# Heads regrouped into neighbouring sets, so that a chunk's projections and gathers split in two halves, in a two-part attention kernel bound by exponentials

## The chip, the cores and the metric

The kernel runs on one core of one Trainium2 chip. The metric is device time of one execution in microseconds (us), and less is better. Before the change it took 406.27 us, the median of 4 runs (405.89 to 406.65).

Five engines work at the same time, each through its own instructions in order: PE (matmul), DVE (VectorE), ACT (ScalarE, here nearly all exponentials), POOL (GpSimd) and SP, which in this kernel issues the DMA transfers. The rows `SPq` in the listings are the issuing of transfers by SP: they too go strictly one after another.

## The reference, cut to what matters

Two attention layers with 32 heads of 20 columns each read their own 2048 x 640 input. Their outputs are put side by side.

```python
# A: four segments of L = 512 rows, causal attention inside the segment plus a linear memory
for s in range(4):
    p = softmax(qs @ ks.T * scale + mask)          # 512 x 512 per head
    a_dot = p @ vs
    pq = phi(qs)                                   # phi(t) = t + 1 if t > 0 else exp(t)
    a_mem = (pq @ M) / (pq @ z + 1e-6)
    o = g * a_mem + (1 - g) * a_dot                # g = sigmoid(beta), one per head
    pk = phi(ks);  M += pk.T @ vs;  z += pk.sum()
A = o @ wo
# B: sliding window of 256 keys, causal
mask = (i - j >= 0) & (i - j < 256)
B = softmax(where(mask, q @ k.T * scale, -1e9)) @ v @ wo
out = concatenate([A, B], axis=-1)
```

## The kernel before

Work goes in eight chunks of 512 rows, in the order A0, B0, A1, B1, A2, B2, A3, B3; here they are called chunk 0 to chunk 7. In a chunk, eight groups of four heads are scored one after the other: PE writes scores `sc`, ACT turns them into exponentials `pt`, PE multiplies `pt` by v, and DVE transposes and normalises. While one chunk is scored, the projections of the next run in between.

A group's four heads lie in four bands of 32 partitions. Which heads make a group decides how much of q and k must exist before the group can be scored. Before, group g holds the heads g, 8+g, 16+g and 24+g:

```python
c0 = DH * (G * j + g)        # proj_direct (chunk 0): head 8j+g; DH = 20, G = 8
h = G * j + g                # the same in the products with v and in the memory
```

These four heads are spread over all 640 columns of q. For chunks 1 to 7 the projection is made in five column blocks of 128 (`m`). Each block is evicted by DVE to `st` and stored to DRAM by SP, then gathered back into the banded layout. The kernel can score no group before the last block has made this round trip:

```python
def bounce(self, m, st, scratch, dst, t, *key):
    def store():
        self.nc.sync.dma_start(out=scratch[m * P:(m + 1) * P, :], in_=st[:, m, :])
        ...                                        # tl: when the store should have landed
        if m > 0: f.at(tl - 150.0, spread)
    def spread():                                  # one gather per band j, four in all
        j = m - 1
        self.nc.sync.dma_start(out=dst[HD * j:HD * j + DH, :, :],
            in_=scratch[GW * j:GW * (j + 1), :].rearrange("(g d) s -> d g s", g=G))
        ...                                        # tl: when the gather should have landed
        if m == self.KT - 1: self.mark(tl, *key)   # only now q (or k) is "known"
...
key = (n, w, e[0]) if n == 0 else (n, w)           # what a score batch of chunk n waits for
need.append(self.done.get(key))
```

The order of the instructions is not written by hand. When the program is built, a small model of the engines' clocks (`Flow`) picks at each step the first thing in a list of jobs whose inputs should be there by then. The order on every engine, SP included, is fixed from then on.

Other parts that the change touches:

```python
# final_job: attention output -> DRAM, transposed back -> output projection -> ot -> DRAM
for tt in range(t0, t1):
    ot = self.wk.tile([P, 640], BF16, name="ot", bufs=2)        # two output buffers
    ...                                                         # 2 x (5 matmuls, eviction to ot)
    def store(ot=ot, r=r): nc.sync.dma_start(out=out2d[r:r + P, col:col + self.D], in_=ot[:])

# norm, chunks with memory: both halves in one multiply, then an add
u = self.wk.tile([P, 2, NB * DH], BF16, name="u", bufs=2)
nc.vector.tensor_tensor(out=self.u, in0=tv[...], in1=rr[...], op=ALU.mult)   # 128 x 640
nc.vector.tensor_tensor(out=dst, in0=self.u[:, 0], in1=self.u[:, 1], op=ALU.add)

# last chunk: every tile masked by a DVE multiply ("fd")
out.append([n, [(g, qt - 2, qt, 1, 0), (g, qt, qt, 1, 128), (g, qt - 1, qt, 1, 256)],
            [("fd", 0, 2)], []])

# start
get_x(0)                                        # transposing load of the first 512 rows
self.wk_A = self.load_w("wk_A", A_wk, pad=HD)
self.wq_A = self.load_w("wq_A", A_wq, pad=HD)
self.load_beta(A_beta)
```

The softmax here doesn't subtract the row's maximum and nothing guards it: scores larger than these inputs give would overflow.

## Time and profile before

| | before |
|---|---|
| time, median of 4 | 406.27 us |
| span of the profiled run | 404.9 us |
| granted PE clock, mean | 0.962 |
| busy: PE / DVE / ACT / POOL | 83 / 78 / 83 / 54 % |

The first lines of the page of before: busy time, share and instruction count of each engine. Below them are two rows that cut the span into 40 slices of 10.1 us, where a digit is the busy share in tenths.

```profile
PE 337.9 (83%) x4580; PEld 159.4 (39%) x4606; DVE 317.5 (78%) x643; ACT 335.4 (83%) x395; POOL 219.8 (54%) x448
...
ACT  1569990987899999998739999999899999999810
POOL 3245650896876677876517667878686664000000
```

PE and ACT have the same share, and the average does not say who bounds the kernel. The ACT row does: it reads 9 nearly everywhere, with dips in the first slices, at slice 6 (counting from 0), at 8 and 9, at 20 and at the end. ACT is saturated in between, so only the dips can be won. They add up to 404.9 - 335.4 = 69.5 us.

The ACT timeline of before names the dips. The columns are start, length, engine, line, operation, tiles and count. The bracket is the idle time before the row and what ended it.

```profile
15.36 9.27 ACT L439 ACTIVATE pt<-sc 128x1024 bf16<-128x1024 f32 x10 [2.67 <-PE sc L427]
27.77 3.77 ACT L439 ACTIVATE pt<-sc 128x1024 bf16<-128x1024 f32 x4 [3.14 <-PE sc L427]
...
70.50 1.51 ACT L439 ACTIVATE pt<-sc 128x768 bf16<-128x768 f32 x2 [9.54 <-PE sc L427]
...
93.90 5.36 ACT L439 ACTIVATE pt<-sc 128x768 bf16<-128x768 f32 x6 [4.43 <-PE sc L427]
```

```profile
207.48 1.94 ACT L439 ACTIVATE pt<-sc 128x1024 bf16<-128x1024 f32 x2 [7.85 <-PE sc L427]
```

```profile
380.75 5.73 ACT L439 ACTIVATE pt<-sc 128x768 bf16<-128x768 f32 x8 [0.83 <-PE sc L427]
```

The reader sees the first score exponential at 15.36 and 3.14 us lost at 24.6, where all of v was projected between two groups. Then 9.54 us are lost from 61 to 70.5 (chunk 1 waits for q), 4.43 us before 93.9, 7.85 us before 207.48, and small holes of 0.83 us in the last chunk. After the last row, 18.46 us pass without exponentials.

The waits of before. The columns are the waiting engine with its tile, what it waited for, the total, how many times and the longest.

```profile
PE m L588 <- DVE ot L594: 9.3, 7, 6.9
PE m L221 <- DMA wk_A<-in_A_wk_dram: 9.0, 1, 9.0
...
DVE ot L594 <- DMA out_dram<-ot: 8.1, 2, 6.5
...
PE m L352 <- DMA pkT<-scr_pk: 5.0, 1, 5.0
```

PE stood 9.0 us for the first weights and 5.0 us for the transposed `pkT`. It stood 6.9 us for DVE's evictions into `ot`, and DVE stood 6.5 us for an output buffer.

The issuing of transfers by SP in before, around the boundary of chunks 0 and 1 and around the hole at 199.6:

```profile
67.68 0.27 SPq L252 DMA_DIRECT2D qB<-scr_qB  x1
```

### The profile page before, as it was taken

Reading aid. Unit: us, or ns where it says so; the run is one execution under the profiler, and the core shown is the slowest. Engines: PE = TensorE matmul, PEld = TensorE weight load, DVE = VectorE, ACT = ScalarE, POOL = GpSimd, SP = SyncE. Lnnn points to the kernel's source line nnn. Section 1 sums busy time; section 2 is a strip of 40 time slices with the busy share of each in tenths; the row PEclk is TensorE's granted clock in tenths of the full one; section 3 lists DMA queues with packets and bytes.
Section 4 is the critical chain, followed back from the end, with each engine's and each line's share of the span. In section 5 each row is a group of like instructions: output and inputs, shape, how many; then the busy total and the mean of one; then the engine's idle time right before and its main releaser. Section 6 shows DMA issues by size and latency. Waiting matters only on the chain.

```text
span 404.9 us, 11529 instructions
## 1 busy us (share of the span) xinstructions
PE 337.9 (83%) x4580; PEld 159.4 (39%) x4606; DVE 317.5 (78%) x643; ACT 335.4 (83%) x395; POOL 219.8 (54%) x448
## 2 busy tenths in 40 slices
PE   1999988967889998887579989798899999998725
PEld 0444334323433443344334344343453344654412
DVE  5666798484897989799556898979867999999851
ACT  1569990987899999998739999999899999999810
POOL 3245650896876677876517667878686664000000
PEclk9999999995999999999869999999999999999986
DMA  7980344898646747155922765427545503173422
GB/s 224 257 300 2 93 127 108 181 190 204 142 126 167 169 111 177 57 169 141 165 82 75 192 161 141 114 87 187 157 115 150 156 24 90 64 177 83 83 70 63
DMA packets 102278, 54.50 MB, mean 135 GB/s; under 512 B 69328, under 2 KB 102224, under 8 KB 102224
## 3 DMA queue, kind: packets, MB, share of 16 engines
q1 hardware_dynamic: 102224, 53.76, 52.5%
q8 instruction: 36, 0.59, 0.6%
q14 instruction: 18, 0.15, 0.1%
HBM read 17.70 MB, written 23.59 MB: 102 GB/s over the span
## 4 chain that ended last, share of the span: by engine, by line
PE 39%; DVE 35%; DMA 10%; ACT 7%; issue 5%; SPq 3%; POOL 1%; DVEq 0%; ACTq 0%
PE m L269 10%; DVE tt L524 8%; PE sc L427 8%; ACT pt L439 7%; PE m L588 6%; PE m L486 5%; PE m L221 5%; PE m L391 5%; DVE st L275 4%; DVE pc L292 4%; DVE pt L455 3%; DVE ot L594 3%; DMA out_dram<-ot 3%; DVE o L544 2%; DVE e L291 2%
## 5 line engine op out<-in xcount | busy, mean ns | idle before, releaser
L439 ACT ACTIVATE pt<-sc 128x1024 bf16<-128x1024 f32 (+1 forms) x360 | 322.2, 1027 | 39.1 <-PE sc L427 38.5
L473 POOL TENSOR_SCALAR_AFFINE_SELECT pt<-pt 128x256 bf16<-128x256 bf16 (+1 forms) x304 | 160.9, 538 | 105.9 <-ACT pt L439 102.2
L524 DVE STREAM_TRANSPOSE tt<-m 128x512 f32<-128x512 f32 x88 | 60.8, 705 | 25.4 <-PE m L486 23.7
L470 POOL TENSOR_SCALAR_AFFINE_SELECT pt<-pt 128x256 bf16<-128x256 bf16 x128 | 62.1, 490 | 12.8 <-ACT pt L439 12.6
L275 DVE CAST st<-m 128x512 bf16<-128x512 f32 x70 | 47.5, 680 | 15.2 <-PE m L269 14.5
L427 PE MATMUL sc<-qB,kB 32*128 32x128 bf16 (+2 forms) x896 | 46.9, 256 | 7.4 <-ACT pt L439 6.2
L594 DVE CAST ot<-m 128x320 bf16<-128x320 f32 x64 | 30.7, 485 | 21.9 <-PE m L588 13.0
L588 PE MATMUL m<-wo_B,oT 128*128 128x320 bf16 x160 | 32.3, 340 | 16.3 <-DMA oT<-scr_o 7.9
L588 PEld LDWEIGHTS <-oT 128*128 128x128 bf16 x320 | 30.3, 103 | 39.6 <-issue 16.1
L391 PEld LDWEIGHTS <-xT 128*128 128x128 bf16 x320 | 29.3, 98 | 27.9 <-issue 17.0
L455 DVE TENSOR_TENSOR pt<-pt,fdmask 128x512 bf16<-128x512 bf16 x96 | 39.1, 433 | 0.0
L427 PE MATMUL sc<-qA,kA 32*128 32x128 bf16 (+3 forms) x512 | 33.5, 300 | 0.6 <-ACT pt L439 0.6
L391 PE MATMUL m<-wv_A,xT 128*128 128x320 bf16 x160 | 28.3, 305 | 6.2 <-DVE tt L524 3.1
L427 PEld LDWEIGHTS <-kB 32*128 32x128 bf16 x896 | 17.4, 92 | 39.8 <-issue 37.4
L588 PE MATMUL m<-wo_A,oT 128*128 128x320 bf16 x160 | 28.8, 305 | 4.6 <-DVE tt L524 2.0
L391 PE MATMUL m<-wBv,xT 128*128 128x320 bf16 x160 | 25.3, 299 | 3.4 <-DVE tt L524 1.5
L269 PE MATMUL m<-xT,wBq 128*128 128x512 bf16 x93 | 23.9, 379 | 2.6 <-DVE tt L524 0.8
L269 PE MATMUL m<-xT,wBk 128*128 128x512 bf16 x92 | 24.7, 381 | 1.2 <-DVE ot L594 0.3
L486 PE MATMUL m<-pt,vA 128*32 128x256 bf16 (+3 forms) x512 | 23.3, 302 | 1.3 <-DVE vB L406 0.8
L551 DVE TENSOR_TENSOR u<-tt,rr 128x640 bf16<-128x640 f32 x24 | 23.2, 965 | 0.5
L544 DVE TENSOR_TENSOR o<-tt,rr 128x320 bf16<-128x320 f32 x40 | 22.1, 553 | 1.1
L427 PEld LDWEIGHTS <-kA 32*128 32x128 bf16 x512 | 9.9, 92 | 31.9 <-issue 31.7
(62 smaller groups left out, 324.0 us busy)
## 6 DMA issues: line engine op xcount, KB each, us to landing
out_dram<-ot SPq DMA_DIRECT2D x32, 160.0 KB
scr_o<-o SPq DMA_DIRECT2D x28, 160.0 KB
scr_kB<-st SPq DMA_DIRECT2D x20, 128.0 KB
kB<-scr_kB SPq DMA_DIRECT2D x16, 160.0 KB
scr_qB<-st SPq DMA_DIRECT2D x20, 128.0 KB
qB<-scr_qB SPq DMA_DIRECT2D x16, 160.0 KB
scr_qA<-st SPq DMA_DIRECT2D x15, 128.0 KB
qA<-scr_qA SPq DMA_DIRECT2D x12, 160.0 KB
```

Source lines behind the costliest of these rows:

```text
L269: nc.tensor.matmul(ps[:, :], lhsT=w_ap[:, kt, m * P:(m + 1) * P], rhs=xT[:, kt, :], start=(kt == 0), stop=(kt == self.KT - 1))
L275: nc.vector.tensor_copy(out=st[:, m, :], in_=ps[:, :])
L391: nc.tensor.matmul(ps[:, 0:320], lhsT=xT[:, kt, tt * P:(tt + 1) * P], rhs=w_ap[:, kt, 320 * hf:320 * hf + 320], start=(kt == 0), stop=(kt ...
L427: nc.tensor.matmul(ps[j // 2][:, j % 2, c0:c0 + nq * P], lhsT=k[rows, g, P * kc:P * kc + P], rhs=q[rows, g, q0 * P:(q0 + nq) * P], start=T ...
L439: nc.scalar.activation(out=pt[:, :, lo:hi], in_=ps[i][:, :, lo:hi], func=ACT.Exp, scale=self.scale)
L455: nc.vector.tensor_tensor(out=pt[:, :, 0:256], in0=pt[:, :, 0:256], in1=self.fd[:].unsqueeze(1).to_broadcast([P, 2, 256]), op=ALU.mult)
L470: nc.gpsimd.affine_select(out=blk, in_=blk, pattern=pat, compare_op=ALU.is_ge, fill=self.zero, base=-1, channel_multiplier=1)
L473: nc.gpsimd.affine_select(out=blk, in_=blk, pattern=pat, compare_op=ALU.is_ge, fill=self.zero, base=0, channel_multiplier=-1)
L486: nc.tensor.matmul(O[HD * j:HD * j + HD, q0 * P:(q0 + nq) * P], lhsT=v[:, vt, VS * h:VS * h + HD], rhs=pts[j // 2][:, j % 2, c0:c0 + nq * ...
L524: self.nc.vector.transpose(out=tt[:, i, :], in_=O[:, :])
L588: nc.tensor.matmul(ps[:, 0:320], lhsT=oT[:, m, tt * P:(tt + 1) * P], rhs=wo[:, m, 320 * hf:320 * hf + 320], start=(m == 0), stop=(m == sel ...
L594: nc.vector.tensor_copy(out=ot[:, 320 * hf:320 * hf + 320], in_=ps[:, 0:320])
```

## The change

The intent is to let every chunk after the first begin when half of its heads are there. Head 4g+j takes the place of head 8j+g. Groups 0 to 3 are then the columns 0 to 319, so they need only the blocks m = 0, 1, 2, and groups 4 to 7 need the rest. Projections of q, k and v become half jobs, gathers come as four per half, and each group has its own mark. Around this core the change also:

- loads the first weights in two parts (352 of 640 columns first),
- carries the output weights through DRAM once to permute their rows,
- splits the normalisation of two-part groups into two multiplies and an add,
- gives the output three buffers,
- hands half of the last chunk's masks to POOL, as two selects each,
- changes some gates: phi of k no longer holds its store back until q of the next chunk is known, and k and q of the later B chunks now wait for phi of the chunk before,
- issues the small load of beta ahead of the weights, not behind them, and puts phi's two DVE operations into stretches where the clock model has DVE idle.

The diff, cut to this core:

```diff
-                c0 = DH * (G * j + g)
+                c0 = DH * (4 * g + j)
...
-            if m > 0:
+            if m in (2, 4):
                 f.at(tl - 150.0, spread)
         def spread():
-            j = m - 1
-            self.nc.sync.dma_start(
-                out=dst[HD * j:HD * j + DH, :, :],
-                in_=scratch[GW * j:GW * (j + 1), :].rearrange("(g d) s -> d g s", g=G))
+            g0 = 0 if m == 2 else 4
+            rows = scratch[4 * DH * g0:4 * DH * (g0 + 4), :]
+            for j in range(4):
+                self.nc.sync.dma_start(
+                    out=dst[HD * j:HD * j + DH, g0:g0 + 4, :],
+                    in_=rows.rearrange("(g j d) s -> j d g s", g=4, j=4)[j])
+            for g in range(g0, g0 + 4):
+                self.mark(tl, n, what, g)
...
+        for half in range(2):
+            for what, w, scr, dst in qk:
+                add(self.qk_job(n, what, half, w, scr, dst, needs[what]))
...
+            add(self.v_job(n, half, *v))
...
-                            key = (n, w, e[0]) if n == 0 else (n, w)
-                            need.append(self.done.get(key))
+                            need.append(self.done.get((n, w, e[0])))
...
-        yield self.known(n + 1, "q")              # pk_job: phi of k, before its store
...
-            ot = self.wk.tile([P, 640], BF16, name="ot", bufs=2)
+            ot = self.wk.tile([P, 640], BF16, name="ot", bufs=3)
...
-                u = self.wk.tile([P, 2, NB * DH], BF16, name="u", bufs=2)
+            u = self.wk.tile([P, NB, DH], BF16, name="u", bufs=2)
...
-                                        (g, qt - 1, qt, 1, 256)], [("fd", 0, 2)], []])
+                                        (g, qt - 1, qt, 1, 256)], [("fd2", 0, 2)], []])
+                if m[0] == "fd2":                 # score_batch: second tile of a pair to POOL
+                    m = ("fd", 0, 2) if i == 0 else ("far", 0, 1)
+                    if i == 1: self.mask(("diag", 128, 1), pt, te)
...
         get_x(0)
-        self.wk_A = self.load_w("wk_A", A_wk, pad=HD)
-        self.wq_A = self.load_w("wq_A", A_wq, pad=HD)
         self.load_beta(A_beta)
+        for nm, w, pad, cut in (("wk_A", A_wk, HD, 352), ("wq_A", A_wq, HD, 352),
+                                ("wv_A", A_wv, 0, 320)):
+            setattr(self, nm, self.load_w(nm, w, pad=pad, cuts=(cut,)))
+            rest.append(self.rest)
```

## The prediction

> **What bounds the kernel now.** ScalarE (the exponentials of the scores). The page gives ACT 335.4 us busy of 404.9 (83%; PE 83%, DVE 78%), but the ACT timeline shows score exponentials back to back through most of 96 to 387 us. Only the holes in ACT can be won, about 69 us. From the ACT timeline and the waits:
> - start: the first score exponential begins at 15.4 us; PE waited 9.0 us for the first projection weights.
> - 3.1 us at 24.6: the whole v projection of chunk 0 sits between the scores of two groups.
> - 9.5 us at 61: chunk 1 can't score any group until all of q is stored and gathered.
> - 4.4 us at 89.5: PE stands 5.0 us on the transposed pkT.
> - 7.9 us at 199.6: DVE waited 6.5 us for an output store (both output buffers full), PE 6.9 us for DVE.
> - about 3 us of small holes in the last chunk; DVE is busy 42.6 of its 46 us, ACT 43.0.
> - 18.4 us after the last exponential: transpose, out-projection, store.
>
> **What the change does.** Head h = 4g+j instead of 8j+g makes four neighbouring groups a contiguous half of q, k and v. Projections, gathers and "ready" marks are split in halves, so a chunk starts when half of its heads are there. Costs: gathers 4 to 8 per tensor, half the size; about 70 more DMA issues at 0.3 to 0.5 us, some 25 us spread over the SP queue; two early round trips of output weights through DRAM. First weights load in two parts; output buffers 2 to 3. In the last chunk half of the 64 masks (one 0.43 us DVE multiply each; 14 us of DVE) go to the idle POOL as two selects of about 0.48 us: per pair of tiles 1.0 us of POOL against 1.5 us of ACT, so POOL keeps up. The two-part normalisation becomes two multiplies of 0.55 us for one of 0.97: +0.14 us x 24, 3.4 us of DVE, mostly hidden.
>
> **On the critical path, estimated.** Start -1.5; v split -2.5; boundary 0/1 -8; pkT -2; output buffers -6; last chunk -2.5. Sum -22.5. I take 2 back for new small waits. Later boundaries show no ACT hole except that at 199.6, so halves win nothing there.
>
> Predicted: 385 us, 374 to 397 in 8 of 10. Faster by over 2%: 0.87; within 2%: 0.10; slower: 0.03.
>
> **Right or wrong if:** ACT busy stays 335 +-3; its longest hole falls from 9.5 to under 4; DVE's wait on output stores falls from 8.1 to under 2; first score exponential near 14; POOL works in the last chunk, with DVE below 35 of 46 us there; the end after the last exponential stays 17 to 19.
>
> **What would make it wrong.** More, later issues on the one in-order SP queue: a gather or output store stuck behind a transpose (about 3 us of issue) makes a new hole. New gates on the k and q projections could move the hole to a later boundary. POOL selects beside two-input DVE multiplies may slow each other: the Trainium skill, "GPSIMD Engine Reference", section "1. Specifications", says that GpSimd shares its SBUF interfaces with VectorE and names contention with instructions that have two SBUF inputs. The trace of before can't show it for the last chunk, where POOL is idle.

## More of the kernel before

```profile
195.33 5.39 SPq L580 DMA_TRANSPOSE oT<-scr_o  x1
200.83 14.61 SPq L600 DMA_DIRECT2D out_dram<-ot  x6
```

The last gather of q for chunk 1 is issued at 67.68, and 2.8 us later the first score exponential runs. At 195.33 a transposing load takes 5.39 us of SP's time, and the six output stores come only behind it.

## The result, and the profile after

| | before | changed |
|---|---|---|
| time, median | 405.8 us (16 runs, 404.34 to 408.05) | 395.1 us (11 runs, 393.04 to 398.31) |
| span of the profiled run | 404.9 us | 392.5 us |
| granted PE clock, mean | 0.962 | 0.990 |
| ACT busy | 335.4 us | 337.1 us |

The ratio is 0.9739, with a 95% interval from 0.9713 to 0.9765: faster, by 2.6%. A ratio here is formed from runs of the two kernels in the same rounds, so it is not quite the ratio of the medians. The record also lists a twelfth run of the changed kernel, 398.55 us, that its median and ratio leave out; with it the mean would be 0.07% higher. The gain is 10.7 us, where 20.5 us were forecast (22.5 less 2 taken back).

The page of the changed kernel, the lines that answer to those of before:

```profile
PE 333.7 (85%) x4574; PEld 156.8 (40%) x4606; DVE 311.5 (79%) x635; ACT 337.1 (86%) x395; POOL 245.7 (63%) x515
...
ACT  1499982999999999899999999999999999999800
POOL 3156650999846668687765666888776665665500
```

The dips at slices 8, 9 and 20 are gone, and of the first slices only two are still low. The dip at slice 6 is still there: it reads 2, with an 8 before it. The end reads nearly as before. POOL now works through the last chunk.

The ACT timeline of the changed kernel:

```profile
15.30 3.77 ACT L479 ACTIVATE pt<-sc 128x1024 bf16<-128x1024 f32 x4 [8.11 <-PE sc L467]
...
61.53 0.63 ACT L309 ACTIVATE e<-kA 128x512 bf16<-128x512 bf16 x1 [3.71 <-DVE pqA L317]
...
67.24 18.30 ACT L479 ACTIVATE pt<-sc 128x768 bf16<-128x768 f32 x22 [3.36 <-PE sc L467]
```

```profile
158.76 20.49 ACT L479 ACTIVATE pt<-sc 128x1024 bf16<-128x1024 f32 x22 [1.70 <-PE sc L467]
```

```profile
366.72 5.75 ACT L479 ACTIVATE pt<-sc 128x768 bf16<-128x768 f32 x8 [1.10 <-PE sc L467]
```

The first score exponential is at 15.30, as before. At the boundary of chunks 0 and 1 the hole is cut up by three small exponentials of phi, so the longest single one is 3.71 us. Between the last score exponential of chunk 0 (ends at 56.49) and the first of chunk 1 (67.24) there are still 10.75 us, against 11.46 before (59.04 to 70.50). The hole at 199.6 has gone; the longest left in chunk 3 is 1.70 us.

The waits of the changed kernel:

```profile
PE m L236 <- DMA wk_A<-in_A_wk_dram: 8.9, 1, 8.9
...
DVE ot L644 <- DMA out_dram<-ot: 4.3, 3, 2.3
```

The wait for the first weights is 8.9 us, unchanged. DVE's wait for output stores fell from 8.1 to 4.3 us, and no wait for `pkT` above 1.1 us is left.

The issuing by SP in the changed kernel, at the boundary, in chunk 3 and at the end:

```profile
61.36 1.44 SPq L269 DMA_DIRECT2D qB<-scr_qB  x4
```

```profile
193.00 0.36 SPq L650 DMA_DIRECT2D out_dram<-ot  x1
...
194.49 0.91 SPq L650 DMA_DIRECT2D out_dram<-ot  x2
...
197.43 2.69 SPq L630 DMA_TRANSPOSE oT<-scr_o  x1
```

```profile
376.82 2.12 SPq L650 DMA_DIRECT2D out_dram<-ot  x2
379.03 1.83 SPq L620 DMA_DIRECT2D scr_o<-o  x4
```

The first-half gather of q is issued at 61.36, not 67.68. In chunk 3 the output stores now go out at 193.00 and 194.49, before the transposing load at 197.43.

The following table is worked out from the two traces. A stage runs from the first score exponential of one chunk to the first of the next, and idle is its length minus ACT's busy time. The lengths add up to the spans.

| stage | before: length / idle | changed: length / idle | length changed by |
|---|---|---|---|
| start | 15.4 / 13.8 | 15.3 / 13.8 | -0.1 |
| chunk 0 | 55.2 / 13.9 | 51.9 / 10.1 | -3.2 |
| chunk 1 | 45.1 / 6.0 | 38.0 / 1.6 | -7.1 |
| chunk 2 | 38.3 / 1.1 | 42.5 / 2.5 | +4.2 |
| chunk 3 | 60.8 / 11.3 | 50.3 / 1.9 | -10.5 |
| chunk 4 | 37.6 / 0.3 | 40.6 / 2.0 | +3.1 |
| chunk 5 | 48.5 / 1.8 | 48.2 / 1.0 | -0.3 |
| chunk 6 | 37.6 / 0.3 | 37.8 / 0.5 | +0.2 |
| chunk 7 | 48.0 / 2.5 | 47.7 / 2.0 | -0.2 |
| end | 18.5 / 18.5 | 20.1 / 20.1 | +1.6 |

The sum is -12.4 us: 14.1 us less idle time and 1.7 us more ACT work. Some of the lengths only moved. In chunk 1, 2.7 us are exponentials of phi that now run in chunk 2, which has 2.8 us more ACT work. Differences below some 2 us in single profiles are scatter. Three kernels with the same order of PE work up to the last chunk (the changed one and the experiments on the output stores and the masks) gave 15.3, 15.7 and 17.0 us for the start, and 50.3, 52.0 and 48.8 us (1.9, 3.5 and 0.6 us idle) for chunk 3.

So three questions stand. Why did the boundary give 0.7 us where 8 were forecast? Why did the start give nothing? And what made chunk 3 so much better, the third output buffer or something else?

### The profile page after: what moved, and what is told of

It reads as the page before. It is cut to its first block, busy times and chain, and to the rows that moved or that the text cites. A ratio compares the mean times of both kernels' runs of the same rounds, so it can differ in the third digit from the quotient of the medians.

```text
span 392.5 us, 11654 instructions
## 1 busy us (share of the span) xinstructions
PE 333.7 (85%) x4574; PEld 156.8 (40%) x4606; DVE 311.5 (79%) x635; ACT 337.1 (86%) x395; POOL 245.7 (63%) x515
## 4 chain that ended last, share of the span: by engine, by line
PE 38%; DVE 35%; ACT 9%; DMA 8%; issue 6%; SPq 2%; POOL 2%; ACTq 0%; DVEq 0%
PE m L291 9%; DVE tt L568 9%; ACT pt L479 8%; PE sc L467 7%; PE m L530 7%; PE m L638 5%; PE m L236 4%; PE m L429 4%; DVE st L297 3%; DVE pc L317 3%; DMA out_dram<-ot 3%; DVE ot L644 3%; DVE u L600 2%; DVE o L593 2%; DVE o L607 2%
## 5 line engine op out<-in xcount | busy, mean ns | idle before, releaser
L517 POOL TENSOR_SCALAR_AFFINE_SELECT pt<-pt 128x256 bf16<-128x256 bf16 (+1 forms) x336 | 174.2, 526 | 121.5 <-ACT pt L479 119.2
L514 POOL TENSOR_SCALAR_AFFINE_SELECT pt<-pt 128x256 bf16<-128x256 bf16 x160 | 76.3, 480 | 5.5 <-ACT pt L479 5.4
L297 DVE CAST st<-m 128x512 bf16<-128x512 f32 x70 | 47.3, 678 | 11.0 <-PE m L291 10.9
L467 PE MATMUL sc<-qB,kB 32*128 32x128 bf16 (+2 forms) x896 | 43.5, 252 | 5.8 <-ACT pt L479 4.7
L638 PE MATMUL m<-wo_B,oT 128*128 128x320 bf16 x160 | 28.8, 312 | 8.8 <-DVE ot L644 4.3
L467 PEld LDWEIGHTS <-kB 32*128 32x128 bf16 x896 | 16.0, 92 | 38.4 <-issue 35.7
L429 PE MATMUL m<-wBv,xT 128*128 128x320 bf16 x160 | 27.1, 299 | 3.1 <-DVE tt L568 1.2
L291 PE MATMUL m<-xT,wBq 128*128 128x512 bf16 x91 | 25.3, 380 | 4.9 <-DVE tt L568 2.7
L499 DVE TENSOR_TENSOR pt<-pt,fdmask 128x512 bf16<-128x512 bf16 x64 | 29.2, 460 | 0.1
L588 DVE TENSOR_TENSOR o<-tt,rr 128x320 bf16<-128x320 f32 x40 | 22.5, 563 | 1.2
L317 DVE SCALAR_TENSOR_TENSOR pc<-st,e 128x512 bf16<-128x512 bf16 x25 | 20.7, 828 | 2.2 <-DMA scr_pq<-pc 1.6
```

The source lines that it names most:

```text
L291: nc.tensor.matmul(ps[:, :], lhsT=w_ap[:, kt, m * P:(m + 1) * P], rhs=xT[:, kt, :], start=(kt == 0), stop=(kt == self.KT - 1))
L297: nc.vector.tensor_copy(out=st[:, m, :], in_=ps[:, :])
L317: nc.vector.scalar_tensor_tensor(out=out, in0=in_, scalar=0.0, in1=e[:], op0=ALU.max, op1=ALU.add)
L429: nc.tensor.matmul(ps[:, 0:320], lhsT=xT[:, kt, tt * P:(tt + 1) * P], rhs=w_ap[:, kt, 320 * half:320 * half + 320], start=(kt == 0), stop= ...
L467: nc.tensor.matmul(ps[j // 2][:, j % 2, c0:c0 + nq * P], lhsT=k[rows, g, P * kc:P * kc + P], rhs=q[rows, g, q0 * P:(q0 + nq) * P], start=T ...
L514: nc.gpsimd.affine_select(out=blk, in_=blk, pattern=pat, compare_op=ALU.is_ge, fill=self.zero, base=-1, channel_multiplier=1)
```

## The experiments

Twelve kernels ran, each beside runs of the kernel before on the same chip. All gave correct results. The ratios are to the kernel before in the same rounds. The changed kernel itself was not run again beside them, so a variant is compared with it through these ratios, and a difference that lies within the intervals is not claimed. One expectation below says that PE is busy 92 to 98% of the time up to 59 us. The windows of the changed kernel show 31.07 of 33 us (94%) from 15 to 48, but only 9.54 of 11 us (87%) from 48 to 59. There DVE is the busy one, with 10.42 of 11 us.

### 1. The third output buffer alone, in the kernel before

SBUF had no room for it: the build then stops, with 57.81 KB needed per partition for the work pool where 56.75 are left. So `u` went down to one buffer. The order of all instructions stays that of before.

```diff
-                u = self.wk.tile([P, 2, NB * DH], BF16, name="u", bufs=2)
+                u = self.wk.tile([P, 2, NB * DH], BF16, name="u", bufs=1)
-            ot = self.wk.tile([P, 640], BF16, name="ot", bufs=2)
+            ot = self.wk.tile([P, 640], BF16, name="ot", bufs=3)
```

> The kernel before with three output buffers instead of two (and one buffer for u, read by the same engine that wrote it, to make room); the order of instructions on every engine is the same. Theory BUFFER (the 7.9 us hole at 199.6 us is DVE waiting for a free output buffer, and the third buffer is what closes it): the hole shrinks to under 2 us and the time falls by 6 us, to about 399.8 (ratio 0.985). Rival QUEUE (the output stores themselves are late, because they stand behind a transpose of 5.4 us on the SP queue; the third buffer fills up as well, and only the new order of the whole program closes the hole in the changed kernel): the hole stays above 4 us and the time falls by under 3 us (ratio above 0.992).

Measured: 402.56 us, ratio 0.9909 (0.9884 to 0.9934), 0.9% faster, between the two expectations and nearer to QUEUE's. The waits, SP's issuing and the ACT timeline around the hole of chunk 3, in this kernel:

```profile
DVE ot L594 <- DMA out_dram<-ot: 5.7, 1, 5.7
```

```profile
195.75 6.70 SPq L580 DMA_TRANSPOSE oT<-scr_o  x1
202.56 11.45 SPq L600 DMA_DIRECT2D out_dram<-ot  x6
```

```profile
209.34 1.94 ACT L439 ACTIVATE pt<-sc 128x1024 bf16<-128x1024 f32 x2 [7.42 <-PE sc L427]
```

The hole is still there: 7.42 us against 7.85. With three buffers DVE fills one more and then stands for 5.7 us, because the output stores start only at 202.56, behind a transposing load that occupies SP from 195.75 for 6.70 us. What the buffer brought came elsewhere: in the last chunk, whose idle time went from 2.5 us to 0.03, and 1 us at the end. So the third buffer alone doesn't close this hole, and what DVE waits for in it is a store that stands behind the transposing load in SP's order.

### 2. Two output buffers in the changed kernel

```diff
-            ot = self.wk.tile([P, 640], BF16, name="ot", bufs=3)
+            ot = self.wk.tile([P, 640], BF16, name="ot", bufs=2)
```

> The changed kernel with two output buffers again, the order of instructions the same. Theory BUFFER: the hole comes back, +5 to +8 us, ratio to before 0.987 to 0.994. Rival QUEUE: under +2 us, ratio to before 0.974 to 0.979.

Measured: 413.23 us, ratio 1.017 (1.0136 to 1.0204): 1.7% slower than before the change, beyond what either theory expected. In the traces the order of instructions on every engine is that of the changed kernel. The waits of this kernel, and SP's issuing in chunk 3:

```profile
DVE ot L644 <- DMA out_dram<-ot: 19.1, 6, 4.1
...
PE m L548 <- DVE ot L644: 9.0, 3, 3.7
```

```profile
193.20 3.32 SPq L650 DMA_DIRECT2D out_dram<-ot  x2
```

DVE stands 19.1 us for output stores, and the products with v in the last chunk stand 9.0 us behind DVE. The last chunk takes 59.0 us instead of 47.7, with holes of 3.07, 3.57 and 3.67 us in ACT, and chunk 3 has 4.3 us idle instead of 1.9. Experiments 1 and 2 also separate the buffer from the order. ACT's idle time, from one profile each:

| chunk 3 / last chunk | two buffers | three buffers |
|---|---|---|
| old order | 11.3 / 2.5 | 9.8 / 0.03 |
| order of the changed kernel | 4.3 / 12.7 | 1.9 / 2.0 |

In chunk 3 the new order takes away 7.0 us even with two buffers: output stores go out from 193.20 there, ahead of the transposing load (199.34). The buffer takes away 1.5 to 2.4 us, hardly more than the scatter. In the last chunk it is the buffer that counts, above all in the new order.

The same buffer is worth 0.9% in the old order and 4.4% (1.017 / 0.9739) in the new one. The new order doesn't give a gain in the total without the buffer, and the buffer gives little of it without the new order. The halved `u` of the split normalisation is part of what makes room for it.

### 3. The changed kernel, with whole chunks as the gate of the scores

Everything stays split, but a score batch of chunks 1 to 7 waits again for all of q and k.

```diff
-                            need.append(self.done.get((n, w, e[0])))
+                            need.append(self.done.get((n, w, e[0]) if n == 0 else (n, w)))
```

> The changed kernel, but a chunk's scores may start only when all of its q and k are gathered, as before; the projections and gathers stay split. Theory HALVES HELP A LITTLE: between the last score exponential of chunk 0 and the first of chunk 1 there are 10.7 us in the changed kernel against 11.5 before; without the early start the second half arrives some 10 us later or more (the last gather of q is issued at 80.4 instead of 62.5), so the hole grows by 8 to 16 us and the ratio to before is 0.99 to 1.02. Rival HALVES ARE EMPTY (the PE would have done the same projections first, so only their order changes): the hole grows by under 3 us, ratio 0.974 to 0.982.

Measured: 422.48 us, ratio 1.0402 (1.0378 to 1.0427), slower than either theory expected. The ACT timeline and SP's issuing in this kernel:

```profile
92.75 1.51 ACT L479 ACTIVATE pt<-sc 128x768 bf16<-128x768 f32 x2 [27.91 <-PE sc L467]
```

```profile
83.58 1.49 SPq L269 DMA_DIRECT2D qB<-scr_qB  x4
```

The hole is 27.91 us; between the score exponentials of chunks 0 and 1 it is 35.3 us, 24.6 more than in the changed kernel, where 8 to 16 more were expected. The second-half gather of q is issued only at 83.58, behind the stores of phi and two transposing loads, and lands at 89.0; before the change the last part of q was issued at 67.68 and landed at 70.67. In the changed kernel itself all of q is there at 84.05. This is the key to the boundary. In the changed kernel the whole of q comes some 13 us later than before (84.05 - 70.67), and scoring by halves buys that delay back, plus the 3.3 us by which chunk 1 now starts earlier. (The gate also reordered the later instructions, from about 67 us on, so the 24.6 us are not the worth of the halves alone.) The forecast counted the half as if the rest of the pipeline had stayed as it was.

### 4. First weights ahead of the first transposing load

```diff
-        get_x(0)
-        self.load_beta(A_beta)
         for nm, w, pad, cut in (("wk_A", A_wk, HD, 352), ("wq_A", A_wq, HD, 352), ...):
             setattr(self, nm, self.load_w(nm, w, pad=pad, cuts=(cut,)))
             rest.append(self.rest)
+            if nm == "wk_A":
+                get_x(0)
+            if nm == "wq_A":
+                self.load_beta(A_beta)
```

> The changed kernel, with the first part of the k weights issued before the transposing load of x, and beta after the first part of the q weights. In the changed kernel that part of the weights is issued at 4.1 us and landed at 8.9, though it is 55% of what landed at 9.0 before. Theory ISSUE (the start waits for DMAs that are issued one after the other on one queue, not for bytes of the weights): x lands near 6.2 instead of 5.6 us and the weights earlier than that, so PE starts near 6.3 instead of 8.9, the first score exponential comes 2 to 2.7 us earlier (near 12.8), and 1.5 to 2.7 us of it arrive at the end: ratio to before 0.967 to 0.971. Rival BYTES (the DMA engines are full from the start, whatever the order): PE starts at 8 us or later, under 1 us is won, ratio 0.972 or more.

Measured: 391.94 us (389.28 to 395.12), ratio 0.9654 (0.961 to 0.9697). This is the fastest kernel; the interval lies clear of that of the changed kernel. Only the order on SP differs: on the other engines it is the same. The timeline of its first microseconds:

```profile
0.81 0.45 SPq L135 DMA_DIRECT2D wk_A<-in_A_wk_dram  x1
...
1.31 3.50 SPq L153 DMA_TRANSPOSE xT<-in_A_x_dram  x1
...
6.85 3.73 PE L236 MATMUL m<-xT,wk_A 128*32 128x512 bf16 x40 [6.85 <-DMA xT<-in_A_x_dram]
...
12.89 3.77 ACT L479 ACTIVATE pt<-sc 128x1024 bf16<-128x1024 f32 x4 [2.52 <-PE sc L467]
```

The weights are issued at 0.81 and the input at 1.31. PE begins at 6.85, now released by the input, and the first score exponential is at 12.89, 2.4 us earlier. The scatter of the start doesn't cover this: the four kernels with early weights read 12.9 to 13.8 us, the other eight with the changed order 15.3 to 17.3. In the changed kernel the same first 55% of the weights were issued at 4.12, because the transposing load ahead of them took 2.64 us of SP's time and beta another 0.57. They landed at 8.88, against 8.96 for the full weights of before, which were issued at 3.55. So the smaller part was on its way for 4.76 us instead of 5.41, and beta, which the change put ahead of it, took nearly all of that back. What the first wait hangs on is mostly the place of the weights in SP's order: issued first, they land at 4.49.

The Trainium skill, "DMA: Bandwidth & Descriptors", section "Issuing engines are not separate DMA queues", says that issuing from several engines at once only saves the sequencer's time for starting a transfer, "which is usually small relative to the DMA itself". For the first plain loads here that holds (0.4 to 0.6 us of issue, 3.4 to 5.4 us to land, in the three traces). It does not hold for the first transposing load: 2.64 of 4.8 us in the changed kernel and 3.50 of 5.5 in this one, and in the changed kernel the weights stand behind it.

### 5. Half of chunk 1's first projections pulled ahead in the job list

The first theory of the boundary was that the first-half projections of chunk 1 only start late, behind the projections of chunk 0, so that moving them ahead closes the hole. The rival, called WORK, was that the engines have that much to do before chunk 1 can start, whatever comes first.

```diff
         for half in range(2):
             for what, w, scr, dst in qk:
                 add(self.qk_job(n, what, half, w, scr, dst, needs[what]))
+                if n == 1 and half == 0:   # mark_job, set elsewhere: ahead of chunk 0's projection of k, group 6
+                    self.jobs.insert(self.jobs.index(self.mark_job), self.jobs.pop())
```

> The changed kernel with the first-half k and q projections of chunk 1 placed before the projections of the last two head groups of chunk 0. In the changed kernel those six tiles start at 48.1 us and are evicted at 59.0, the last gather lands at 65.3, the first score stands in PE's order behind eight other matmuls until 66.8. Theory CHAIN (the hole between chunk 0 and 1, 10.7 us from the last exponential to the first, is the latency from eviction to score, which can be hidden behind the exponentials of the last two groups): a hole of 3 to 6 us opens inside chunk 0, the one at the boundary falls below 4, the first score exponential of chunk 1 comes 3 us or more earlier than at 67.2, ratio to before 0.962 to 0.968. Rival WORK (PE is busy 92 to 98% of 9 to 59 us, DVE 95% of 48 to 59, so what is put first delays the rest): the first score of chunk 1 moves by under 1.5 us and the ratio stays 0.970 to 0.979.

Measured: 395.48 us, ratio 0.9751 (0.9719 to 0.9782), no different from the changed kernel. The ACT timeline of this kernel:

```profile
52.56 3.77 ACT L479 ACTIVATE pt<-sc 128x1024 bf16<-128x1024 f32 x4 [7.59 <-PE sc L467]
```

The first exponential of chunk 1 comes at 65.10, 2.1 us earlier (CHAIN expected 3 or more, WORK under 1.5), but chunk 0 itself has got a hole of 7.59 us. Chunks 0 and 1 together take 92.5 us against 90.0. The hole has only moved, and the ratio is the one that WORK expected.

### 6. Phi of chunk 0 held back until half of q is known

This was meant to test whether DVE's work on phi (two operations per piece, eight pieces, from 48.8 us on) makes the first half of q late.

```diff
         else:                              # pk_job, chunk 0
             yield self.known(0, "k")
+            yield self.known(1, "q", 0)
```

> The changed kernel, but the eight exp-and-max pieces over k of chunk 0 (for the memory; about 1 us of DVE each, between 48.8 and 67.8 us) wait until the first half of q of chunk 1 is gathered. Theory DVE (in the hole at the boundary of chunks 0 and 1 the DVE, busy 10.4 of 11 us from 48 to 59, delays the evictions of the projections by these pieces): the last eviction of the first half comes 3 us or more earlier than at 59.0, the first score exponential of chunk 1 near 64 instead of 67.2, ratio 0.964 to 0.970, if the memory's pkT isn't then late. Rival PE (the projections themselves are the pace): under 1 us at the boundary; and the later pieces may open a hole in chunk 2, where pkT is waited for: ratio 0.973 or more.

Measured: 406.58 us, ratio 1.0033 (1.0 to 1.0066), the whole gain lost. The first half of q was no faster for it: 11.6 us from the start of its projections to the last eviction against 10.9 in the changed kernel, although DVE was busy only 7.9 of 13 us from 46 to 59. So DVE's share in phi is not what made it late; PE was busy 12.0 of these 13 us. But the hole grew to 14.80 us, and the order of SP changed with it:

```profile
60.92 2.89 SPq L621 DMA_DIRECT2D scr_o<-o  x4
63.91 0.47 SPq L260 DMA_DIRECT2D scr_qB<-st  x1
...
67.30 1.48 SPq L269 DMA_DIRECT2D qB<-scr_qB  x4
```

The third block of q is evicted by 61.66, but its store (63.91) now stands behind four stores of `scr_o`, and the gather comes at 67.30, not 61.36. The experiment cannot say how much DVE's relief alone is worth. The later gather goes with 4.0 us more at the boundary. The larger part of the loss lies in chunk 1, where the phi work now falls and ACT is idle for 8.1 us instead of 1.6; that was not traced.

### 7. The last output stores issued by ACT

At the end, the stores of the last tile's attention output (379.03) stood behind output stores (376.82, 2.12 us). Here output stores that come after the last score batch are issued by ACT, which has nothing left to do.

```diff
-                nc.sync.dma_start(out=out2d[r:r + P, col:col + self.D], in_=ot[:])
+                (nc.scalar if self.tail else nc.sync).dma_start(
+                    out=out2d[r:r + P, col:col + self.D], in_=ot[:])
```

> The changed kernel, with the output stores that come after the last exponential in program order issued from the ACT queue instead of SP. In the changed kernel the last normalised tile is ready at 376.8 us, but its store to scratch is issued at 379.0, behind two output stores; the time from the last exponential to the end is 20.1 us against 18.5 before. Theory QUEUE ORDER: that end falls by 1.5 to 3 us, ratio 0.966 to 0.970. Rival BACKLOG (the end is long because out-projections put off by the earlier stages, some 70 matmuls after the last exponential, are done there): under 1 us, ratio 0.972 or more.

Measured: 394.57 us, ratio 0.9736 (0.969 to 0.9783). The end took 18.2 us in the profile instead of 20.1, but the total can't be told from the changed kernel's 0.9739. Whether the 1.9 us are a gain stays open.

### 8. All masks of the last chunk on DVE again

```diff
-                                        (g, qt - 1, qt, 1, 256)], [("fd2", 0, 2)], []])
+                                        (g, qt - 1, qt, 1, 256)], [("fd", 0, 2)], []])
```

A guard was added to keep the order of the last transposes valid (`final_job` waits until its `oT` exists).

> The changed kernel with all masks of the last chunk on DVE again (and one line that keeps the order of the last output jobs legal). Theory SMALL (ScalarE sets the pace of the last chunk: ACT is idle only 1.9 of its 47.7 us with POOL masks and was idle 2.5 of 48.0 before): last chunk and end together longer by 1 to 3 us, ratio 0.976 to 0.982. Rival DVE-BOUND (with the larger backlog of output work, DVE at 42.6 of 46 us before has no room): longer by 4 us or more, ratio 0.984 or more.

Measured: 394.1 us, ratio 0.9727 (0.9692 to 0.9762). The masks on POOL gain nothing: not even the 1 to 3 us of SMALL are lost without them. Two views of the last chunk, for the changed kernel and then for this one. The first is the row of the window (length, then busy time of PE, PEld, DVE, ACT and POOL, clock, DMA share and GB/s), and the second is the group of DVE's mask multiplies (count, busy, mean ns).

```profile
324.70:372.40 47.70, 43.03 (x893) 25.80 (x893) 39.92 (x95) 45.75 (x65) 28.12 (x63) 1.00 0.46 116
```

```profile
L499 DVE TENSOR_TENSOR pt<-pt,fdmask 128x512 bf16<-128x512 bf16 x31 | 14.6, 472 | 0.0
```

```profile
324.80:370.60 45.80, 42.92 (x882) 25.08 (x882) 44.94 (x120) 45.59 (x65) 0.64 (x1) 1.00 0.48 121
```

```profile
L499 DVE TENSOR_TENSOR pt<-pt,fdmask 128x512 bf16<-128x512 bf16 x62 | 23.6, 412 | 0.0
```

With POOL idle DVE is busy 44.94 of 45.8 us, and ACT is still at 45.59. With half the masks on POOL, DVE is at 39.92 and ACT is no faster. DVE was close to full but not what ACT waited for once the third output buffer was there. Experiment 1 already showed the last chunk without holes, with all masks on DVE. (In single profiles ACT's idle time in the last chunk scatters with POOL masks too, from 0.3 to 2.3 us in the other variants with three output buffers.) Also, a DVE mask takes 472 ns on average beside POOL's selects and 412 ns without them: 19 of the 31 took at most 419 ns, the other 12 took 499 to 650. This agrees with the Trainium skill, "GPSIMD Engine Reference", section "1. Specifications", that names contention of the two engines when a DVE instruction has two SBUF inputs. The price here is 15% on the mean of these instructions.

### 9. Two groups of chunk 1 without the round trip

If the round trip through DRAM sets the boundary, projecting the groups 0 and 1 of chunk 1 directly into the bands, as chunk 0 does, should close the hole. Direct projection costs more PE time. The first gather brings only groups 2 and 3 then.

```diff
+        if n == 1:                         # seed, before the halves
+            for g in range(2):
+                for what, w, scr, dst in qk:
+                    add(self.proj_direct(1, w, self.xs[1], dst, g, what, tx))
...
-            rows = scratch[4 * DH * g0:4 * DH * (g0 + 4), :]
+            ga = 2 if n == 1 and m == 2 else g0
+            rows = scratch[4 * DH * ga:4 * DH * (g0 + 4), :]
...                                         # ga in place of g0 in the gathers and marks too
```

> The changed kernel, but q and k of the first two head groups of chunk 1 are projected straight into their places, as in chunk 0, with no store and gather; the half's gather brings the other two groups. PE does 80 column-tiled matmuls more (about 4.2 us by those of chunk 0). Theory CHAIN (most of the 10.7 us between the last score exponential of chunk 0 and the first of chunk 1 is the way of the half through the SP queue and DRAM: last eviction at 59.0, gather issued at 61.4, landed at 65.3, scored at 66.8): the first score exponential of chunk 1 follows that of chunk 0 within 2 us, ten exponentials (9.3 us) run before the gathered groups are there, a hole of 3 to 5 us may stay behind them, and 3 to 6 us are won at the end: ratio 0.959 to 0.967. Rival WORK (PE has no time to spare before 67 us, so 4.2 us of extra work cost what they bring): the exponentials start earlier, but by the first of chunk 2 less than 1.5 us is left of it, ratio 0.971 to 0.980.

Measured: 409.25 us, ratio 1.0073 (1.0022 to 1.0125), slower than both theories expected. The ACT timeline, SP's issuing and the scores on PE in this kernel:

```profile
87.97 4.49 ACT L480 ACTIVATE pt<-sc 128x768 bf16<-128x768 f32 x5 [19.07 <-PE sc L468]
```

```profile
67.85 2.66 SPq L621 DMA_DIRECT2D scr_o<-o  x4
70.61 3.81 SPq L370 DMA_DIRECT2D scr_pk<-pqA  x4
74.46 2.63 SPq L270 DMA_DIRECT2D qB<-scr_qB  x4
```

```profile
87.34 0.51 PE L468 MATMUL sc<-qB,kB 32*128 32x384 bf16 x4
```

The first exponentials of chunk 1 come at 57.83 without any hole, as meant. Then 19.07 us are lost. The third store of q had landed by 69.2, but the gather is issued only at 74.46, behind `scr_o` (67.85, 2.66 us) and `scr_pk` (70.61, 3.81 us). That is 5.2 of the 19 us. The last of these gathers lands at 78.57, and then PE comes to the scores only at 87.34: its order has other projections first, and these wait in turn for DVE, which stands 3.6 us for a store of `scr_kB`. From the first score exponential to the first of chunk 2 it is 110.1 us, against 90.0 in the changed kernel.

### 10. The same, with the weights first

The edits are those of experiments 4 and 9 together.

> Both the order of the first loads (weights of k before x, won 2.4 us at the start and 0.85% in all, by itself) and the direct projection of two groups of chunk 1. If the two gains add: theory CHAIN, ratio 0.950 to 0.959, 386 to 389 us; rival WORK: 0.963 to 0.971.

Measured: 406.68 us, ratio 1.0026 (0.998 to 1.0073). The hole is 19.29 us, so it doesn't depend on the start. The earlier start is worth about 2.6 us here too (406.68 against 409.25), within the spread of the two.

### 11. Weights first, two direct groups, and a gate on the stores that stood in front

If SP's order makes the hole of experiment 9, a gate on the stores of phi and of the attention output of chunk 0 should shrink it: they wait until the second half of q is known.

```diff
         yield f.dve                        # pk_job, after phi and before its stores
+        if c == 0:
+            yield self.known(1, "q", 7)
...
         yield t                            # final_job, before its stores
+        if n == 0:
+            yield self.known(1, "q", 7)
```

The guard of experiment 8 is in it too.

> As the run with both the early weights and the direct projection of two groups, but the stores of chunk 0's output and of its memory keys are held back until q of chunk 1 is gathered, so on the SP queue each gather of chunk 1 stands right behind the stores it needs. In the direct run without this the q gather of the first half was issued at 74.5 us though its last store had landed at 69.2, with eight such stores in front of it, and a hole of 19 us was left. Theory SP ORDER (what is won or lost at the boundary is set by what stands in front of the gather on the one in-order queue): the hole behind the first ten exponentials of chunk 1 is 7 us or less, the gather of q is issued within 1 us of its last store's landing, and the ratio is 0.950 to 0.963. Rival WORK (the PE pays for the direct projections anyway): the hole closes, but others open up to chunk 2, ratio 0.966 or more.

Measured: 404.09 us, ratio 0.9953 (0.9911 to 0.9995). SP's issuing and the ACT timeline in this kernel:

```profile
66.67 1.43 SPq L270 DMA_DIRECT2D qB<-scr_qB  x4
```

```profile
74.60 8.50 ACT L482 ACTIVATE pt<-sc 128x768 bf16<-128x768 f32 x10 [8.22 <-PE sc L470]
```

The gather goes out at 66.67, right after its last store landed, and the hole falls from 19.3 to 8.2 us. The 7 us or less that the theory asked for were narrowly missed. So SP's order, and what hangs on it, set most of that hole: the gathers land at 69.46, and 4.7 us still pass until PE comes to the scores at 74.14. Yet other holes opened (3.65 us before 109.7, 2.51 us before 85.6, 26.6 us at the end instead of 20), and from the first score exponential to the first of chunk 2 it is 95.9 us, still more than 90.0. On the total, WORK's ratio was right: in this order two more groups by the dear route don't pay.

### 12. Weights first and the gate, without direct groups

The edits are those of experiment 4 and the gate of experiment 11.

> The early weights and the held-back stores, without the direct projection: the control. By itself the early order of the weights had ratio 0.9654. In the changed kernel the gather of q already stood right behind its stores (issued at 61.4, landed store 61.3), so theory SP ORDER expects no change at the boundary (hole 10 to 11.5 us) and a ratio of 0.960 to 0.970; if the memory's keys come too late, a hole of some us opens in chunk 1 or 2 and the ratio is above 0.970.

Measured: 398.15 us (4 runs), ratio 0.9821 (0.9792 to 0.9851), where 0.960 to 0.970 was expected. The boundary did not move: 10.7 us from chunk 0's last score exponential to chunk 1's first, as with the weights first alone. That part was expected. But chunk 4 has 6.2 us idle instead of 2.0, chunk 5 2.4 instead of 0.9 and chunk 1 3.4 instead of 2.1. Holding chunk 0's stores back costs more than the order at the boundary gives. Why it shows as late as chunk 4 was not traced.

## Why the prediction was right or wrong

The time, 395.1 us, lies in the range of 374 to 397 and the change is faster by more than 2%, as forecast. The size is just over half of it: 10.7 us of 20.5. In part that is luck: the boundary fell 7.3 us short, while chunks 3 and 1 gave 5.8 us more than forecast, chunk 3 for a reason that the forecast did not have. Term by term:

| term of the forecast | forecast | measured |
|---|---|---|
| start | -1.5 | -0.1 |
| v split | -2.5 | -2.5 |
| boundary of chunks 0 and 1 | -8 | -0.7 |
| pkT (idle of chunk 1) | -2 | -4.4 |
| output buffers (idle of chunk 3) | -6 | -9.4 |
| last chunk (idle) | -2.5 | -0.5 |
| end | 0 | +1.6 |
| new small waits (idle of chunks 2, 4, 5, 6) | +2 | +2.4 |
| ACT's own work, chunk 0 left out | 0 | +1.1 |
| sum | -20.5 | -12.4 |

The measured sum is that of the two profiled spans (the terms are rounded); the medians differ by 10.7. The v split and the boundary are read as lengths: from the first to the last score exponential of chunk 0, and from there to the first of chunk 1.

What was right: ACT bounds the kernel, and its busy time stayed (337.1 against "335 +-3"). The v split is worth its hole. The chunk-0 part from first to last score exponential went from 43.7 to 41.2 us, and the hole of 3.14 us is gone; no experiment undid the v split alone. The wait for `pkT` is gone, and the small new waits came as large as set aside. That chunk 1's idle fell by 4.4 us, not 2, may have a second part. The granted clock in before was 0.50 from 94 to 101 us, right after PE's standing; in the changed kernel it was 1.00 there. This was not separated.

The step that failed is "boundary 0/1 -8", with "its longest hole falls from 9.5 to under 4". By the letter the longest single hole is 3.71 us, since three phi exponentials fall into the gap, but the gap between score exponentials is 10.75 us against 11.46. The forecast took the hole as the time by which half of q comes earlier than the whole. The traces show three things in its place:

- The start and the end of the gap both moved. Chunk 0 ends 2.5 us earlier by the v split. That was counted as a gain of its own, and it lengthens the wait for q by the same amount. This double counting is read from the sum of the stages and is argued, not tested.
- The half comes 5.3 us earlier than the whole, not 8 or more. The last eviction of what the first group needs falls from 64.9 to 59.0 us. After it there is a chain that doesn't halve: the last eviction at 59.0, the store landed at 61.34, four gathers issued from 61.36 to 62.8, the last landed at 65.34. (A landing is read from the semaphore updates in the trace: each gather of 20 rows shows one update 0.4 to 0.6 us after its issue and ten later, and the last of the ten is the landing. The Trainium skill explains this in "DMA: Bandwidth & Descriptors", section "Why a DMA increments its semaphore by 16 and not by 1": a transfer on fewer than 16 DMA engines gets the missing counts at once from the sequencer. The trace agrees.) Before, the last gather landed at 70.67 and the scores had waited on it for 0.34 us. Now the score follows only at 66.78, behind eight projection matmuls that PE's order put ahead of it.
- Earlier would not have been free. PE is busy 94% from 15 to 48 us and DVE 95% from 48 to 59. When the projections are pulled ahead (experiment 5) the hole opens inside chunk 0, and when two groups are projected directly (9 to 11) it opens after them. The halves are needed in the new order (experiment 3: a hole of 27.91 us without), but most of what they bring goes to repay the delay of the whole of q in that order.

"Start -1.5" failed because it took the bytes of the weights for the main cause. Fewer bytes shortened their way by 0.65 us, and beta's load, now ahead of them, took 0.57 us of it back. They wait for SP behind a transposing load; experiment 4 moved them and won 2.4 us.

"Output buffers -6" was right in sign, but its reason was wrong. It read DVE's wait for an output buffer as a lack of buffers. Experiment 1 shows that the third buffer leaves 7.42 of the 7.85 us, and the listing of SP shows why: the stores that would free the buffers stood behind a transposing load. In the changed order they go first. Experiment 2 shows that the new order takes away 7.0 of the 9.4 us even with two buffers. It was not an intent of the change, and which part of the change reordered the stores was not tested. DVE's wait on output stores fell to 4.3 us, not under 2.

"Last chunk -2.5" failed because it was put down to DVE's masks. The holes belonged to the output buffers (experiment 1: 0.03 us idle with three), and the masks on POOL brought nothing (experiment 8). "DVE below 35 of 46 us" was 39.9 of 47.7, in part because the remaining masks got 15% dearer on average.

"The end stays 17 to 19" was 20.1. The order at the end delays the last tile's stores, and experiment 7 shortened the end but could not show a gain in time.

The best version is the changed kernel with the first weights ahead of the first input: 391.94 us, 3.5% faster than before.

## What to carry to other kernels

When a change lets a stage start earlier, work out the new start from the whole chain (last producer, store, gather, place in the consumer's order) and from the new end of the stage before, and do not subtract the old hole. On an in-order queue of transfers, look first at what stands in front of the one that is late: a transposing load that occupies the issuer for 3 to 7 us explained the start and the hole of chunk 3, and neither fewer bytes nor one more buffer alone removed them. A part that is worth little by itself can be indispensable in another order (the third output buffer: 0.9% alone, 4.4% in the changed kernel), so undo parts in the new kernel as well as adding them to the old one.

## What the Trainium skill lacked or had wrong

- "DMA: Bandwidth & Descriptors", section "DMA Transpose (X-bar)", gives no issue time for a transposing load of this size from DRAM. Here a 512 x 640 one mostly occupied SP for 2.5 to 4.7 us. It was 5.4 to 9.2 us in two places, the second input at the start, with the weights still moving, and the load before the hole of chunk 3. (The record of that last one also carries a wait for PE, which the trace doesn't separate from the issue.) A plain transfer mostly took 0.3 to 0.6 us. The sentence in "Issuing engines are not separate DMA queues" that issue time is usually small does not fit such loads: it delayed the start (2.4 us) and the stores in the hole of 7.42 to 7.85 us in chunk 3.
- "GPSIMD Engine Reference", section "1. Specifications", names the contention with DVE but no size. Here a 128 x 512 bf16 multiply on DVE with two SBUF inputs took 412 ns on average with POOL idle and 472 ns beside POOL's selects, where 12 of 31 took 499 to 650 ns.
